# 64-token chunks from the third block on, one pass of K over identity and values, and a new instruction order, in a fused RetNet and RWKV channel-mix kernel

## The chip, the cores and the metric

The kernel runs on one core of one Trainium2 chip. The metric is the device time of one run in microseconds; the median of three runs before the change is 153.27 us (152.85 to 153.36).

## What is computed

Four sequences of 768 tokens with 8 heads of 64 pass through a retention layer, whose output is the input of a gated channel mix (d_model 512, d_ff 1024):

```python
for t in range(S):
    state = gamma[None, :, None, None] * state + np.einsum('bhd,bhe->bhde', k[:, :, t], v[:, :, t])
    y[:, :, t] = scale * np.einsum('bhd,bhde->bhe', q[:, :, t], state)
...
xk = mu_k * x + (1.0 - mu_k) * x_prev
xr = mu_r * x + (1.0 - mu_r) * x_prev
k = np.maximum(xk @ w_k, 0.0)
v = k * k @ w_v
r = 1.0 / (1.0 + np.exp(-(xr @ w_r)))
return (r * v)
```

## The kernel before, in words

The tokens are cut into 12 blocks of 256, three for each sequence. A block's retention is computed in chunks: scores of the tokens of a chunk among themselves (masked), plus what the state carried into the chunk gives, plus the chunk's own addition to the state. Decay is folded into constants: V is scaled once by powers of gamma, and the output is scaled back, so that the masks hold only zeros and ones.

Three sets name how each block is cut. Blocks in `HALF` use four chunks of 64 tokens, with TensorE split into 64x64 quadrants, four of which work at once. Blocks in `WIDE` (2 to 5) use two chunks of 128 tokens, with 64x128 and 128x64 tiles, two at once. Blocks 0 and 1 use 128-token chunks of interleaved tokens. Blocks in `WHOLE` turn (transpose) q and k 128 tokens at a time, the others 64.

**The order is written out.** The scheduler is off. `ORDER` is one list of words; each is a step, its engine (`~v` VectorE, `~a` ScalarE, `~p` GpSimd, `~s` SyncE; none means TensorE or a fixed engine) and the PSUM banks (`@`) of its result. Every engine runs its own words strictly in the order of the list, so a word that waits holds all later words of its engine. GpSimd and SyncE issue the DMAs, in the same way. The first number of a word is the block:

- `lq`, `lk`, `lv` (L223): loads of q, k and v of a block; `wk`, `wr`, `wv`: loads of weights. Input buffers are rings of four blocks. `ck`, `cq`: casts of the first half block.
- `Tq`, `Tk` (L265) and `Eq`, `Ek` (L241, through L285 and L297): TensorE turns q and k into PSUM; ScalarE copies them to SBUF as f16.
- `vs` (L253): V scaled, as f16.
- `S` (L312, L324): scores; `M` (L347, L354): scores times mask.
- `C` (L359, L373): products of K and V, the chunks' additions to the state; `U` (L419): running sums of the state over chunks; `G` (L424): the decay from block to block.
- `I` (L441): the first half of the state's part of the output; `Y` (L456, L470): the scores' part, and for most blocks the second half of the state's part; `J`: that half by itself. They accumulate in the same two banks. `D` (L507, L514): the output, scaled, into `xT`.
- `dx` (L529) and `X.n.w.j` (L558, for block 0 L552 with `t`, L542): difference to the token before, and the two mixes (w = 0 for xk, w = 1 for xr), one for each of four 128-channel slices j.
- `K` (L582, L572), `Qa` (L591), `Qb` (L599, L603): keys, relu, square; `R` (L612), `s` (L618): gate and sigmoid; `V` (L624; `Vc` L642): values; `O` (L630; `Oc` L649): their product; `st`, `sc`: stores.
- `cm` (L680): masks and identity; `gy` (L718, L728): powers of gamma; `mu`, `mt`, `me`: the mix weights; `z` (L703, L710): products of zeros on TensorE that nobody reads.

`GROUPS` joins blocks 3 and 4, 6 and 7, 9 and 10 for the channel mix: their words `X`, `K`, `Qa` and `Qb` (with the first block's number) treat both blocks at once. So `R.10` needs all four `X.9.1.j`, and `K.9.g` all four `X.9.0.j`.

Of the kernel before, what the change touches and what calls it, by code (L numbers as in the profile page):

```python
# [799 lines left out]
```

## Time and profile before

| | |
|---|---|
| median of three runs | 153.27 us |
| span of the profiled execution | 151.4 us |
| TensorE (PE) busy | 143.4 us, 2426 matmuls |
| VectorE (DVE) busy | 127.8 us, 212 instructions |
| ScalarE (ACT) busy | 103.6 us, 195 instructions |
| GpSimd (POOL) busy | 55.3 us, 65 instructions |
| HBM read, written | 24.16 MB, 6.29 MB |

The profiled execution has no time of its own besides its span; the 1.9 us between the span and the median of the timed runs is what lies around the span. PE is the matmuls, PEld the weight loads that run beside them. Matmuls are pipelined and the ends of their bars are modelled, so that what a group of them costs is read from the distance between starts, or from the chain. In a group's row stand line, engine, operation, output <- input, shapes, count, then busy time and mean length of one, then the idle time just ahead of them and what ended it. The chain of work is followed back from the last instruction; a share in it belongs to whatever the end waited for at that time. The tenths show the busy share in 40 equal slices of 3.8 us.

### The profile page before, as it was taken

How to read it: one execution, taken by the hardware profiler on the slowest of the kernel's cores; microseconds unless marked ns; L12 is line 12 of the kernel's file. 1: busy time of each engine (PE TensorE's matmuls, PEld its weight loads, DVE VectorE, ACT ScalarE, POOL GpSimd, SP SyncE). 2: the span in 40 equal slices, each digit the busy share in tenths (PEclk: the TensorE clock that was granted, in tenths of full speed). 3: DMA queues.
4: the chain of work that ended last, by engine and by line, in shares of the span. 5: the costliest groups of instructions: out<-in, count | busy, mean ns of one | idle time of the engine just before them, and what ended most of it. 6: DMA issues, size and time to landing. Idle time of an engine off the chain costs nothing.

```text
span 151.4 us, 5541 instructions
## 1 busy us (share of the span) xinstructions
PE 143.4 (95%) x2426; PEld 82.8 (55%) x2426; DVE 127.8 (84%) x212; ACT 103.6 (68%) x195; POOL 55.3 (37%) x65
## 2 busy tenths in 40 slices
PE   7878799999999999999999999999999999999991
PEld 3345487757754554547465564548456444655450
DVE  7886999999989999999999999999799999400432
ACT  3565979899844795779567786999604756839420
POOL 7953998577957309996710000000000000000000
PEclk9999999999999999999999999999999999999999
DMA  5999999999999999999999019301000005500433
GB/s 140 219 229 197 207 231 192 168 251 212 196 167 202 233 262 107 256 300 198 231 173 126 7 38 283 105 35 45 0 4 0 4 0 211 205 0 0 148 133 139
DMA packets 45624, 22.16 MB, mean 146 GB/s; under 512 B 37400, under 2 KB 41248, under 8 KB 45600
## 3 DMA queue, kind: packets, MB, share of 16 engines
q0 software_dynamic: 38704, 14.42, 74.5%
q1 hardware_dynamic: 6592, 7.21, 14.3%
q8 instruction: 19, 0.31, 0.8%
q10 hardware_dynamic: 304, 0.18, 0.4%
q14 instruction: 5, 0.04, 0.1%
HBM read 24.16 MB, written 6.29 MB: 201 GB/s over the span
## 4 chain that ended last, share of the span: by engine, by line
PE 73%; DMA 12%; POOL 11%; issue 1%; DVE 0%; POOLq 0%
PE ps L624 27%; PE ps L572 14%; DMA v<-in_v_dram 12%; PE ps L612 12%; PE ps L582 8%; PE ps L278 3%; POOL q L235 3%; POOL k L230 2%; PE ps L441 2%; POOL vs L253 2%; POOL v L230 2%; PE ps L366 1%; PE ps L462 1%; PE ps L642 1%; PE ps L318 1%
## 5 line engine op out<-in xcount | busy, mean ns | idle before, releaser
L624 PE MATMUL ps<-wv,k2s 128*128 128x512 f16 x184 | 44.1, 380 | 0.0
L591 ACT ACTIVATE kr<-ps 128x512 f32<-128x512 f32 x48 | 27.9, 594 | 12.5 <-PE ps L582 6.5
L624 PEld LDWEIGHTS <-k2s 128*128 128x128 f16 x184 | 17.1, 98 | 18.9 <-ACT k2s L603 0.4
L630 DVE SCALAR_TENSOR_TENSOR os<-ps,rs 128x512 f32<-128x512 f32 x23 | 15.6, 684 | 11.9 <-ACT rs L618 9.4
L612 PE MATMUL ps<-wr,xr 128*128 128x512 f16 x96 | 23.5, 379 | 0.0
L582 PE MATMUL ps<-xk,wk 128*128 128x256 f16 x192 | 23.2, 273 | 0.0
L572 PE MATMUL ps<-xk,wk 128*128 128x512 f16 x96 | 23.0, 379 | 0.0
L618 ACT ACTIVATE rs<-ps 128x512 f32<-128x512 f32 x24 | 13.6, 597 | 12.9 <-PE ps L612 12.1
L230 POOL DMA_DIRECT2D k<-in_k_dram x20 | 17.8, 903 | 10.3 <-PE ps L384 6.7
L582 PEld LDWEIGHTS <-wk 128*128 128x128 f16 x192 | 18.1, 98 | 3.7
L241 ACT COPY qT<-ps 128x1024 f16<-128x1024 f16 (+1 forms) x13 | 12.3, 946 | 9.5 <-PE ps L278 7.8
L558 DVE SCALAR_TENSOR_TENSOR xr<-dx,mu,xT 128x256 f16<-128x256 f32 (+1 forms) x32 | 17.9, 577 | 0.1
L230 POOL DMA_DIRECT2D v<-in_v_dram x18 | 16.0, 911 | 3.6 <-DMA wr<-in_moe_w_r_dram 1.9
L558 DVE SCALAR_TENSOR_TENSOR xk<-dx,mu,xT 128x256 f16<-128x256 f32 (+1 forms) x32 | 17.0, 579 | 0.2
L354 DVE TENSOR_TENSOR a<-ps,c_sb 128x1024 f16<-128x1024 f32 (+1 forms) x14 | 14.6, 1066 | 0.9 <-PE ps L339 0.6
L603 ACT ACTIVATE k2s<-kr 128x512 f16<-128x512 f32 x24 | 14.8, 631 | 0.3
L612 PEld LDWEIGHTS <-xr 128*128 128x128 f16 x96 | 9.0, 97 | 10.7 <-issue 0.5
L572 PEld LDWEIGHTS <-wk 128*128 128x128 f16 x96 | 9.1, 98 | 10.5
L599 ACT ACTIVATE k2s<-kr 128x512 f16<-128x512 f32 x24 | 14.5, 627 | 0.3
L241 ACT COPY kT<-ps 128x1024 f16<-128x1024 f16 (+1 forms) x13 | 12.2, 945 | 2.2 <-PE ps L272 1.7
L529 DVE TENSOR_TENSOR dx<-xT 128x1024 f32<-128x1024 f32 x11 | 13.4, 1221 | 0.2
L253 DVE TENSOR_TENSOR vs<-v,csm_sb 128x1024 f16<-128x1024 f32 x10 | 12.2, 1217 | 0.2 <-DMA v<-in_v_dram 0.2
(73 smaller groups left out, 165.6 us busy)
## 6 DMA issues: line engine op xcount, KB each, us to landing
out_dram<-os SPq DMA_DIRECT2D x23, 256.0 KB, 2.4
v<-in_v_dram POOLq DMA_DIRECT2D x18, 256.0 KB, 7.7
q<-in_q_dram POOLq DMA_DIRECT2D x11, 256.0 KB, 8.4
k<-in_k_dram POOLq DMA_DIRECT2D x21, 128.0 KB, 8.8
v<-in_v_dram POOLq DMA_DIRECT2D x2, 512.0 KB, 7.2
wk<-in_moe_w_k_dram POOLq DMA_DIRECT2D x2, 512.0 KB, 10.4
...
```

The costliest lines, as they stand in the source:

```text
L230: e.dma_start(out=dst[:, :, i * D : i * D + D], in_=src[:, i * P : i * P + P].rearrange("h p d -> p h d"),)
L241: e.copy(out=out, in_=in_)
L253: e.tensor_tensor(out=VS(n), in0=V32(n).rearrange("p h (i d) -> p i h d", i=2), in1=gks[:, int(half(n) or wide(n)), :, :, None].to_broadca ...
L354: nc.vector.tensor_tensor(out=a_full(n)[:, i, :, j0:j1], in0=pairs(banks("S", n, i, j0))[:, :, j0:j1], in1=(below if wide(n) else causal[: ...
L558: nc.vector.scalar_tensor_tensor(out=XM[w](k)[:, j, t0:t1], in0=DX(k)[:, j, t0:t1], scalar=mu[:, w * NCO + j : w * NCO + j + 1], in1=x[:, ...
L572: nc.tensor.matmul(banks("K", n, g), lhsT=wk16[:, co, g * P : g * P + P], rhs=XM[0](k)[:, co, :], start=(co == 0), stop=(co == NCO - 1),)
L582: nc.tensor.matmul(pz[:, i, :], lhsT=wk16[:, co, fo * P : fo * P + P], rhs=XM[0](k)[:, co, m * TM + t0 : m * TM + t1], start=(i == 0 and c ...
L591: nc.scalar.activation(out=kr, in_=banks("K", n, g, *u), func=AF.Relu)
L603: nc.scalar.activation(out=K2(n)[:, w * g : w * g + w, t0:t1], in_=kr.rearrange("p a t -> p (a t)").rearrange("p (i t) -> p i t", i=w), fu ...
L612: nc.tensor.matmul(banks("R", n, tb), lhsT=XM[1](k)[:, co, t : t + P], rhs=wr16[:, co, :], start=(co == 0), stop=(co == NCO - 1),)
L624: nc.tensor.matmul(banks("V", n, tb), lhsT=K2(n)[:, fo, tb * P : tb * P + P], rhs=wv16[:, fo, :], start=(fo == 0), stop=(fo == NFO - 1),)
L630: nc.vector.scalar_tensor_tensor(out=OS(2 * n + tb), in0=banks("V", n, tb), scalar=1.0 / (KSC * KSC), in1=RS(2 * n + tb), op0=ALU.mult, op ...
```

## The change

Blocks 2 to 5 move into `HALF`: 64-token chunks in quadrants, like the later ones, with no `J` and one mask in place of two, four running sums in place of two, and an output in two pieces. `WIDE` is empty, and `WHOLE` keeps only blocks 0 and 1.

For blocks 2 to 11 (`MERGED`) the words `Tk`, `C` and `Ek` are replaced by `TC.n.i` and `Ec.n.i` (i = 0, 1, the two halves of the chunks). `TC` loads each 64x64 piece of K once as weights and runs 128 columns over it: 64 of an identity that now lies at the front of the buffer of scaled values (`VI`), and 64 of values. One matmul so gives the turned keys and the addition to the state, side by side in f32 PSUM; `Ec` copies the keys' half out, `U` reads the other half. Three identity columns are made in `cm.2`.

A new word `w` (`fence`) lets ScalarE copy a few elements of the banks of `I.n` into a buffer that nobody reads; `Y.n` writes these banks and so waits for it. wk is loaded in three pieces. The order is new throughout; the whole list is replaced, and the diff below shows some stretches of it.

```diff
-HALF = (6, 7, 8, 9, 10, 11)
+HALF = (2, 3, 4, 5, 6, 7, 8, 9, 10, 11)
 EARLY = ((1, 0, 0), (0, 0, 0))
 GROUPS = ((0,), (1,), (2,), (3, 4), (5,), (6, 7), (8,), (9, 10), (11,))
 APART = (0,)
-WHOLE = (0, 1, 2, 3)
-WIDE = (2, 3, 4, 5)
+WHOLE = (0, 1)
+WIDE = ()
+MERGED = (2, 3, 4, 5, 6, 7, 8, 9, 10, 11)
...
-cm.0~v cm.1~v cm.2~v gy.0~v mu~a lv.0~p lq.0.0.2~s lk.0.0.2~s ck.0.0.2~a cq.0.0.2~a z.12@6
-Tq.0.0.2@0 Tk.0.0.2@1 gy.1~v z.1@2 mt@2 Ek.0.0.2~a Eq.0.0.2~a S.0.1.0.2@01 S.0.0.0.2@45 me~a
-lk.0.2.4~p Tk.0.2.4@3 Ek.0.2.4~a lq.0.2.4~p vs.0~v C.0@67 M.0.1.0.2~v U.0.0~v Tq.0.2.4@2 Eq.0.2.4~a
...
-X.8.1.0~v X.8.1.2~v Y.9 D.9~v G.10~a U.11.0~v st.5.0~s U.11.1~v U.11.2~v Qa.8.0~a I.10@23 V.6.1.0@7
-V.6.1.1 O.6.1~v V.6.0.0@4 V.6.0.1 I.11@01 S.11@67 M.11~v dx.9~v V.7.1.0@5 V.7.1.1 Y.10 D.10~v
...
-dx.11~v X.11.1.0~v X.11.1.1~v X.9.1.1~v V.8.1.0@6 K.9.2@3 X.11.0.0~v K.9.6@7 Qa.9.6~a V.8.1.1
-Qa.9.2~a Qb.9.2~a X.11.0.3~v K.9.5@7 K.9.3@3 K.9.0@2 Qa.9.0~a Qb.9.6~a V.8.0.0@0 V.8.0.1 Qb.9.0~a
-Qa.9.5~a Qb.9.5~a Qa.9.3~a O.7.1~v st.7.1~s X.9.1.2~v X.11.0.1~v O.6.0~v K.9.7@1 R.8.1@7 s.8.1~a
-K.9.1@5 R.8.0@7 X.9.1.3~v X.11.0.2~v st.6.1~s O.8.1~v R.9.1@4 R.9.0@6 K.11.0@3 K.11.3@2 s.8.0~a
-Qa.9.1~a Qb.9.1~a Qb.9.3~a V.10.0.0@5 V.9.0.0@7 Qa.11.0~a Qb.11.0~a Qa.11.3~a s.9.0~a K.9.4@6
-R.10.0@2 Qa.9.7~a X.11.1.3~v st.6.0~s K.11.1@1 Qa.11.1~a Qa.9.4~a K.11.2@3 Qb.9.7~a Qb.9.4~a
-Qa.11.2~a X.11.1.2~v O.8.0~v st.7.0~s st.8.1~s st.8.0~s V.9.1.0@1 V.10.1.0@6 s.10.0~a V.9.1.1
-V.10.0.1 s.9.1~a O.9.1~v st.9.1~s Qb.11.2~a Qb.11.3~a O.10.0~v st.10.0~s R.10.1@4 V.9.0.1 s.10.1~a
-O.9.0~v R.11.1@4 V.10.1.1 Qb.11.1~a V.11.0.0@7 R.11.0@5 s.11.0~a st.9.0~s Vc.11.1.1@1 s.11.1~a
-O.10.1~v st.10.1~s Oc.11.1.1~v V.11.0.1 O.11.0~v st.11.0~s sc.11.1.1~a Vc.11.1.0@4 Oc.11.1.0~v
-sc.11.1.0~s
...
+gy.0~v lk.0.0.2~s ck.0.0.2~a cm.2~v cm.0~v gy.1~v lv.0~p cm.1~v z.4@0 z.4@1 z.2@0 Tk.0.0.2@0 mu~a
+lq.0.0.2~s cq.0.0.2~a vs.0~v lq.0.2.4~p lk.0.2.4~p Ek.0.0.2~a Tq.0.0.2@1 Eq.0.0.2~a z.3@7
+S.0.1.0.2@23 Tq.0.2.4@0 Eq.0.2.4~a M.0.1.0.2~v S.0.0.0.2@45 M.0.0.0.2~v Tk.0.2.4@1 C.0@67 U.0.0~v
+Ek.0.2.4~a S.0.1.2.4@23 I.0@01 U.0.1~v w.0~a S.0.0.2.4@45 M.0.1.2.4~v lk.1~p lq.1~p Tk.1@6 Ek.1~a
+lv.1~p z.2@7 Tq.1@2 Eq.1~a wk.0.1~p M.0.0.2.4~v wk.1.2~p Y.0 z.1@3 S.1.1@67 D.0~v G.0~a S.1.0@45
+mt@2 me~a M.1.1~v wk.2.4~p t.0.0.3~a t.0.1.3~a t.0.0.0~a t.0.0.2~a vs.1~p z.4@3 C.1@23 M.1.0~v
+U.1.0~v z.3@7 I.1@01 X.0.0.3~v X.0.0.2~v t.0.1.0~a X.0.0.0~v t.0.0.1~a X.0.0.1~v w.1~a t.0.1.1~a
+U.1.1~v Y.1 lq.2~p z.1@5 K.0.0@4 Qa.0.0~a G.1~a K.0.2@2 Qa.0.2~a t.0.1.2~a D.1~v K.0.3@0 dx.1~v
+X.1.0.1~v Tq.2@67 X.1.0.0~v Eq.2~a X.1.0.3~v lv.2~p X.1.0.2~v vs.2~v X.1.1.0~v Qa.0.3~a X.0.1.0~v
+X.1.1.3~v K.0.1@1 K.1.3@2 lk.2~p Qb.0.0~a wr~p TC.2.0@45 U.2.0~v X.1.1.1~v TC.2.1@67 Ec.2.0~a
+U.2.1~v lv.3~p Qb.0.3~a Ec.2.1~a Qa.0.1~a Qb.0.1~a K.1.0@3 K.1.1@0 Qa.1.0~a S.2@45 Qb.1.0~a
+X.0.1.2~v Qa.1.1~a X.1.1.2~v R.1.1@1 U.2.2~v I.2@67 w.2~a Qa.1.3~a Qb.1.1~a R.1.0@3 s.1.0~a M.2~v
+Y.2 Qb.1.3~a X.0.1.1~v s.1.1~a X.0.1.3~v vs.3~v K.1.2@0 Qa.1.2~a D.2~v dx.2~v lk.3~p TC.3.0@45
...
+X.2.1.2~v TC.4.0@01 wv.0~p lq.5~p Ec.4.0~a D.3~v U.4.0~v TC.4.1@45 U.4.1~v U.4.2~v Ec.4.1~a U.4.3~v
+Qa.2.1~a wv.1~p K.2.3@3 S.4@67 X.2.1.0~v Qb.1.2~a I.4@01 V.1.0.0@2 Qa.2.3~a V.0.0.0@3 w.4~a
+X.2.1.3~v Qb.2.3~a Tq.5@45 M.4~v dx.3~v Y.4 D.4~v X.2.1.1~v V.0.1.0@6 G.4~a V.1.1.0@7 dx.4~v V.1.0.1
...
+K.3.5@0 Qa.3.5~a st.0.0~s Qb.3.5~a X.3.1.2~v D.5~v O.2.0~v dx.5~v X.5.0.1~v K.3.7@6 R.4.1@7 I.6@23
+Qa.3.7~a Qb.3.7~a st.2.0~s s.4.1~a TC.7.0@45 Ec.7.0~a U.7.0~v w.6~a U.7.1~v st.2.1~s TC.7.1@01
+U.7.2~v X.5.0.0~v R.3.0@6 Ec.7.1~a U.7.3~v X.5.0.2~v R.4.0@7 s.3.0~a s.4.0~a Qb.3.0~a R.3.1@4
+X.5.0.3~v Y.6 s.3.1~a Qb.3.2~a lk.8~p D.6~v dx.6~v S.7@67 M.7~v I.7@01 K.5.2@5 K.5.1@4 Qa.5.1~a
+V.3.1.0@2 lv.8~p vs.8~v V.4.1.0@3 w.7~a Y.7 D.7~v dx.7~v X.6.0.2~v lq.10~p Tq.10@67 X.6.0.3~v
...
+Ec.11.0~a Qb.6.5~a K.8.0@2 Qa.8.0~a R.7.1@3 s.7.1~a U.11.0~v st.4.1~s U.11.1~v S.11@45 Qb.6.4~a
+I.10@01 V.6.0.0@2 U.11.2~v I.11@67 w.10~a Y.10 M.11~v I.9@45 X.8.1.2~v w.11~a Y.11 X.8.1.3~v D.10~v
+w.9~a Y.9 K.8.1@3 Qa.8.1~a Qb.8.1~a D.11~v D.9~v dx.9~v V.7.0.0@0 dx.10~v Qb.8.0~a X.9.0.0~v
...
+X.11.0.1~v X.11.0.3~v V.7.1.1 O.6.1~v K.9.3@7 Qa.9.3~a X.11.1.2~v s.8.1~a st.6.1~s K.9.7@5 O.7.1~v
+Qb.9.3~a Qa.9.7~a X.11.0.2~v R.8.0@1 Qb.8.2~a X.9.1.0~v st.7.1~s K.9.4@6 Qb.8.3~a Qa.9.1~a Qb.9.1~a
+K.9.2@5 s.8.0~a X.9.1.1~v st.7.0~s X.9.1.3~v R.10.1@7 R.10.0@2 X.11.0.0~v Qa.9.5~a Qa.9.4~a V.8.1.1
+K.11.1@6 Qa.9.2~a Qb.9.2~a O.8.1~v Qb.9.7~a Qa.11.1~a R.9.1@5 R.9.0@3 V.8.0.1 K.9.6@6 s.9.0~a
+Qb.9.4~a K.9.0@3 X.11.1.3~v Qa.9.0~a K.11.3@0 K.11.0@1 Qb.9.0~a s.10.1~a Qa.9.6~a V.10.0.0@3
+st.6.0~s V.9.1.0@6 O.8.0~v Qa.11.0~a K.11.2@1 st.8.0~s V.9.0.0@4 Qb.9.5~a V.10.1.0@7 X.11.1.1~v
+X.11.1.0~v Qa.11.2~a R.11.1@1 Qb.9.6~a st.8.1~s V.9.1.1 s.10.0~a s.9.1~a O.9.1~v V.9.0.1 V.10.1.1
+O.9.0~v Qb.11.2~a Qa.11.3~a Qb.11.1~a st.9.0~s O.10.1~v st.10.1~s Qb.11.0~a V.11.0.0@0 V.10.0.1
+st.9.1~s R.11.0@2 Qb.11.3~a V.11.0.1 O.10.0~v st.10.0~s Vc.11.1.1@3 Vc.11.1.0@4 s.11.0~a O.11.0~v
+st.11.0~s s.11.1~a Oc.11.1.1~v Oc.11.1.0~v sc.11.1.1~a sc.11.1.0~s
...
+    def VS(n):
+        return VI(n)[:, 1:].rearrange("p (i h) d -> p i h d", i=2)
...
-    VS = ring("vs_", 3, [2, H, D], F16)
+    VI = ring("vs_", 3, [2 * H + 1, D], F16)
...
+    def both(n, i):
+        return banks("TC", n, i).rearrange("p u (j x t) -> p u j x t", j=NJ, x=2)
+
+    def turned_state(e, n, i):
+        ps = both(n, i)
+        for j in range(NJ):
+            for u in range(2):
+                for a, h, jo, hp in heads(j):
+                    k = 1 + i * H + h
+                    x = slice(0, 2) if more(n) or not (u and i) else slice(0, 1)
+                    nc.tensor.matmul(
+                        ps[low(a), u, j, x], lhsT=K16(n)[low(u), h, i * D : i * D + D],
+                        rhs=VI(n)[low(u), 0 : k + 1 : k][:, x],
+                        start=(j == 0), stop=(j == NJ - 1), skip_group_check=True,
+                    )
+
+    def turned_k_part(e, n, i):
+        copy(
+            e, KT(n)[:, :, i].rearrange("c j (u p) -> c u j p", u=2), both(n, i)[:, :, :, 0],
+        )
+
     def carried(n, c):
         return TG[c if half(n) else 2 * c](n)
 
     def summed(e, n, c):
-        src = banks("C", n)
-        if half(n):
-            src = src[:, c % 2, c // 2 * NJ * D : (c // 2 + 1) * NJ * D]
-            last = c == 3
+        last = c == (3 if half(n) else 1)
+        if merged(n):
+            src = both(n, c // 2)[:, c % 2, :, 1]
...
+    def fence(e, n):
+        us = slice(0 if half(n) or not first(n) else 1, 2)
+        e.copy(out=fenced[:, us], in_=pairs(banks("I", n))[:, us, :, 0:C:W])
...
-            ((step, 2, ALU.is_ge), (below, 0, ALU.is_ge)),
+            ((step, 2, ALU.is_ge), (below, 0, ALU.is_ge))
+            + tuple((VI(i)[:, 0], 2, ALU.is_equal) for i in range(3) if MERGED),
...
-    def load_wk(e, h):
-        f = slice(h * dff // 2, (h + 1) * dff // 2)
+    def load_wk(e, a, b):
+        f = slice(a * dff // 4, b * dff // 4)
```

More of the change, by code (lines that the diff above doesn't have):

```diff
@@ L158 @@
     zero = const.tile([P, P], F32, name="zero")
-    mu8 = const.tile([P, P], F32, name="mu8")
+    fenced = const.tile([P, 2, NJ, 2], F32, name="fenced")
     mu = const.tile([P, 2 * NCO], F32, name="mu")
@@ L177 @@
     count = OS(3)[:, 0:P]
+    mu8 = OS(2)[:, 0:P]
     ctx.enter_context(tc.manual_schedule())
@@ L213, in first, with merged @@
         return n % NB == 0
+    def merged(n):
+        return n in MERGED
     def more(n):
```

75 lines of the change are left out of this document (31 added, 44 removed).

## Prediction

> **What bounds the kernel now.** I read the page's totals first, then the busy tenths, then the chain.
>
> ```profile
> span 151.4 us, 5541 instructions
> PE 143.4 (95%) x2426; PEld 82.8 (55%) x2426; DVE 127.8 (84%) x212; ACT 103.6 (68%) x195; POOL 55.3 (37%) x65
> ...
> PE   7878799999999999999999999999999999999991
> ...
> DVE  7886999999989999999999999999799999400432
> ACT  3565979899844795779567786999604756839420
> ...
> PE 73%; DMA 12%; POOL 11%; issue 1%; DVE 0%; POOLq 0%
> ```
>
> The chain names PE for 73% of the span and DVE for nothing. Yet the tenths show DVE as full as PE in nearly every slice until the 33rd, after which it is half idle. So I cut the span where the DVE stretch begins and ends. 19.78 us is where DVE starts D.1, and 127.78 us is where it ends X.9.1.3, the last of the four products that the gate matmuls R.9 and R.10 need. The columns are length, then busy time of PE, PE's weight loads, DVE, ACT and POOL.
>
> ```profile
> 0.00:19.78 19.78, 15.31 (x317) 8.91 (x318) 16.19 (x44) 11.81 (x24) 14.74 (x20) 1.00 1.30 198
> 19.78:127.78 108.00, 107.59 (x1994) 62.54 (x1993) 104.81 (x159) 80.05 (x149) 40.54 (x46) 1.00 0.96 145
> ```
>
> In the middle stretch DVE is busy 104.81 of 108.00 us; only 3.19 us are idle. PE is busy too, but it can put V and R groups, whose inputs are ready long before, wherever it likes. After 127.78 DVE has little left (the zeros and fours that end its line of tenths) and PE works on. The seam shows how tight the two are:
>
> ```profile
> 127.04 0.74 DVE L558 SCALAR_TENSOR_TENSOR xr<-dx,mu,xT 128x512 f16<-128x512 f32 x1
> ```
>
> ```profile
> 127.19 1.89 PE L612 MATMUL ps<-wr,xr 128*128 128x512 f16 x8
> ```
>
> ```profile
> 127.36 2.70 PE ps L612 x12
> ...
> 141.32 0.86 PE ps L624 x4
> ...
> 147.37 0.89 PE ps L642 x8
> ...
> 148.28 0.42 DVE os L649
> ```
>
> The twelve L612 matmuls are R.8.0, R.9.1 and R.9.0 at 0.86 us each, so R.9.1 starts near 127.19 + 0.86 = 128.05, about 0.3 us after its last input. From there PE has 20.2 us left, to 148.26. **Two engines bind, one after the other: DVE up to X.9.1.3, then PE to the end.** A change gains only if it brings this seam forward, or leaves less PE work behind it. The span ends 151.4 - 148.26 = 3.1 us after PE; the median of 153.27 lies 1.9 us above the span. I keep both, since the last two half products and stores are the same.
>
> **PE, part by part.** Dense work is unchanged (the same K, R and V groups). The attention groups change shape:
>
> ```profile
> 56.01 0.55 PE ps L331 x16
> ...
> 60.96 0.57 PE ps L478 x16
> ...
> 70.20 0.38 PE ps L318 x32
> ...
> 95.09 0.38 PE ps L366 x32
> 95.47 0.26 PE ps L318 x32
> ```
>
> ```profile
> 12.60 0.61 PE L272 MATMUL ps<-c_sb,k 128*64 128x128 f16 x16
> 13.14 0.64 PE L489 MATMUL ps<-a,vs 64*64 64x128 f16 x32
> 13.62 0.28 PE L441 MATMUL ps<-qT,tg 64*64 64x128 f16 x4
> ```
>
> A group entered from dense work costs about 0.12 us more than the same behind another small one (0.38 against 0.26). Scores in blocks 2 to 5 go from 0.55 to 0.38, and the value products from 0.57 to about 0.38 (L462 has the shape of L366): 4 x 0.36 = 1.4 us. Transposes in blocks 2 and 3 go from 0.54 (start to start) to 0.26: 4 x 0.28 = 1.1. One pass of K has 32 matmuls of 128 columns at about 0.44 (L489's starts are 0.48 apart with the switch) in place of two passes of 0.26: 0.08 x 10 = 0.8. That is about 3.3 us. The zeros rise from 23 to 24 units of 0.22: -0.2. PE is lighter by about **3.0 us**, bounds 2.1 (no gain in the K pass) and 3.5.
>
> [...]
>
> **DVE up to X.9.1.3.** Durations by form:
>
> ```profile
> L253 DVE TENSOR_TENSOR vs<-v,csm_sb 128x1024 f16<-128x1024 f32 x10 | 12.2, 1217 | 0.2 <-DMA v<-in_v_dram 0.2
> L354 DVE TENSOR_TENSOR a<-ps,c_sb 128x1024 f16<-128x1024 f32 x10 | 12.0, 1219 | 0.3 <-PE ps L331 0.2
> ...
> L419 DVE TENSOR_TENSOR tg<-ps,tg 128x256 f16<-128x256 f32 x20 | 8.4, 418 | 0.6 <-ACT tg L424 0.4
> ...
> L507 DVE TENSOR_TENSOR xT<-ps,gy_sb 128x512 f32<-128x512 f32 x12 | 8.3, 689 | 0.7
> ...
> L514 DVE TENSOR_TENSOR xT<-ps,gy_sb 128x1024 f32<-128x1024 f32 x6 | 7.3, 1218 | 1.4 <-PE ps L441 1.2 <-PE ps L478 0.2
> ...
> L680 DVE TENSOR_SCALAR c_sb<-os,csm_sb 128x64 f16<-128x64 f32 x1 | 0.2, 235 | 0.0
> ```
>
> Blocks 2 to 5 lose one mask each (-4 x 1.22 = -4.88), gain two running sums each (+8 x 0.418 = +3.34), and write their outputs in two pieces instead of one (4 x (2 x 0.689 - 1.218) = +0.64). vs.3 moves from POOL to DVE (+1.22). Three identity columns are new (+0.70). One X.11 moves from before the seam to after it (the 128x256 form, some -0.48). Sum: **+0.5 us**. So the engine that carries the seam is not relieved at all: 121.0 us of work (16.19 + 104.81) become 121.5. One duration has no row: the running sums of merged blocks read 64 columns out of every 128. If that costs nothing, 0.418 holds; were it as dear as a mix of the same 256 elements (0.48), 37 sums would add 2.2 us. I take 0.418, since the output's L507 also walks in strides and costs no more per element than the mask's L354.
>
> What can move the seam is DVE's idle time:
>
> ```profile
> 3.11 1.62 DVE L680 TENSOR_SCALAR c_sb<-os,csm_sb 128x128 f16<-128x128 f32 x5
> ...
> 4.77 2.57 DVE L728 TENSOR_TENSOR gy_sb<-gy_sb,csm_sb 128x4 f32<-128x4 f32 x8
> ...
> 10.87 1.89 DVE L354 TENSOR_TENSOR a<-ps,c_sb 128x512 f16<-128x512 f32 x3 [0.60 <-PE ps L339]
> 13.95 1.23 DVE L514 TENSOR_TENSOR xT<-ps,gy_sb 128x1024 f32<-128x1024 f32 x1 [1.19 <-PE ps L441]
> ...
> 109.88 1.23 DVE L347 TENSOR_TENSOR a<-ps,c_sb 128x1024 f16<-128x1024 f32 x1 [0.72 <-PE ps L318]
> ```
>
> At the start the new order computes powers (L728) before masks (L680). The identity that the first transposes need then comes some 2 us later in DVE's queue, near 6.6 us; but DVE, busy until about 9 us with the same words in any order, needs the first scores no earlier. The four masks of block 0 then stand closer together. Of 0.60 + 1.19 us I let 1.0 go (an estimate; bounds 0 and 1.8). The rest stays, since D.0 still waits for Y.0. The wait of 0.72 goes: S.11 is now issued ahead of V.6.0.0, not behind four V groups. Of the other 2.5 us in the middle stretch I change nothing; bounds are 1.3 gained, and the waits below.
>
> The seam then comes at 127.78 + 0.5 - 1.0 - 0.7 = **126.6**. Behind it the new order has more PE work than the old one: R.10.1, which needs X.9.1.3, and 25 groups after it, 26 x 0.865 = 22.5 us, where 23 groups (20.2 us) stood behind R.9.1. So the lighter PE shows as work that had to be left for the tail, because DVE doesn't come sooner. DVE's rest doesn't break that tail: four products and two results (some 3.3 us) stand before R.11.1's last input, 16 groups (13.8 us) on PE. PE ends at 126.6 + 0.1 + 22.5 = 149.2, the span at 152.3, the run at **154.2 us**, 0.9 above the median.
>
> **What I cost at nothing.** ACT:
>
> ```profile
> L591 ACT ACTIVATE kr<-ps 128x512 f32<-128x512 f32 x48 | 27.9, 594 | 12.5 <-PE ps L582 6.5 <-PE ps L572 6.0
> ...
> L241 ACT COPY kT<-ps 128x1024 f16<-128x1024 f16 x11 | 11.0, 1010 | 0.5 <-PE ps L278 0.5
> ...
> L241 ACT COPY kT<-ps 128x512 f16<-128x512 f16 x2 | 1.2, 586 | 1.7 <-PE ps L272 1.7
> ...
> L694 ACT COPY mu<-ps 128x8 f32<-128x8 f32 x1 | 0.2, 183 | 0.0
> ```
>
> Twenty half copies of keys replace ten whole ones (20 x 0.59 - 10 x 1.01 = +1.8 us; from an f32 source no row shows them, but the f16 form has 0.586 and L591's f32 form 0.594), and twelve fences add 12 x 0.18 = 2.2. ACT's middle stretch goes from 80 to about 84 of 108 us, so the throughput fits. The waits may not. Each fence makes Y.n wait for ACT, and behind Y.n in PE's queue stand dense groups; ahead of the fence in ACT's queue stand squares and copies of 0.6 us. Loads keep their bytes and pieces, only wk comes in three pieces instead of two (+0.8 us of POOL, which loses vs.3's 1.9). V now matters more: the pass over K needs both K and scaled V, where the turned keys needed K alone.
>
> ```profile
> 25.54 10.37 DMA v<-in_v_dram
> ...
> 35.98 1.91 POOL vs L253
> ```
>
> V of block 3 landed at 25.54 + 10.37 = 35.91 with 10 MB queued up to it (blocks 0 to 3, q and k of block 4, wk, wr). The new order queues 8 MB; at the same 0.28 MB per us that is 29 us, in time for its place in DVE's queue near 30.
>
> **Rivals.** (1) *The lighter PE shows.* If it did in full: 153.27 - 3.0 = 150.3. DVE's work forbids that: with 1.8 us gone at the start and all but 1.2 us of the middle's idle time, the seam is at 127.78 + 0.5 - 1.8 - 2.0 = 124.5, so PE ends at 147.1 and the run at 152.1. For it: PE has slack to serve DVE early. Against: three engines are nearly full at once. (2) *Fences stall PE* and so the scores that DVE masks. Between I and Y the order puts dense groups in most blocks, but little in blocks 1, 5, 9 and 11; 4 x 0.5 us (half an ACT instruction, the copy, the way back) = 2.0: 156.2. It decides once ACT runs more than one dense group (0.86 us) behind. (3) *V comes late* in blocks 3 and 4. Keys, copies, scores and mask (0.44 + 0.59 + 0.59 + 0.38 + 1.22 = 3.2 us) then follow it, where they ran beside it; two thirds exposed give 156.3.
>
> **How the numbers follow.** No change means within 0.3%, 152.8 to 153.7, about what a measurement of this kernel can tell. Forecast 50% (faster 2, same 11, slower 37), its own range 153.0 to 155.4. Rival 1 25% (faster 22, same 3), rival 2 18% and rival 3 7% (all slower). Faster 0.24, same 0.14, slower 0.62. The range runs from 151.8 (rival 1 with only 0.9 us idle left in the middle) to 156.4 (rivals 2 and 3).
>
> **What would show it.** Right: DVE still over 95% busy between D.1 and X.9.1.3, the seam at 126 to 127.5, and 22.5 us of unbroken PE behind it. Rival 1: seam before 125. Rival 2: PE or its weight loads waiting for the fence line, several times 0.3 us or more. Rival 3: DVE idle at L253, waiting for V's DMA between 25 and 45 us. Wrong altogether: a seam somewhere else, such as R.10.1 not starting on X.9.1.3, or a DVE instruction whose duration changes with its new strided source in PSUM (the running sums read every second 64 columns).

## The result and the profile after

The changed kernel takes **166.44 us** (median of 4 runs, 165.45 to 168.66), the kernel before 153.28 beside it (152.85 to 153.36). The ratio is 1.084, 95% interval 1.080 to 1.088. Ratios, and differences between two kernels below, leave out runs that are over 1.5% above the fastest of their kernel; medians and ranges are of all runs. The forecast was 154.2 with a range up to 156.4: the sign is right, the size is not, 13.2 us where 0.9 was expected.

The page of the changed kernel (its profiled execution took 166.31 us). First the totals, then four rows of tenths, then the chain by engine:

```profile
span 164.5 us, 5668 instructions
PE 145.8 (89%) x2459; PEld 81.9 (50%) x2459; DVE 129.0 (78%) x224; ACT 103.6 (63%) x217; POOL 54.2 (33%) x65
...
PE   7789728898398999979899999999899999999992
...
DVE  6996759999558998998699999999999997230342
...
PEclk9999999999969999999999999999999999999999
DMA  6999999999999996972999006801100006030063
...
PE 42%; DVE 28%; ACT 11%; issue 10%; DMA 5%; POOL 2%; DVEq 0%; ACTq 0%; POOLq 0%
```

Before, both PE and DVE showed nearly unbroken nines from the sixth slice on. Now both have holes in the first twenty slices, and the chain, which named DVE for nothing, changes hands all the time. "issue", time in which an engine waits for nothing that the profile shows, has grown from 1% to 10%.

Where along the span is the time lost? I cut both executions where D.5 ends and where X.9.1.3 ends (the seam). Columns: length, then busy time of PE, PE's weight loads, DVE, ACT and POOL, granted clock. First before, then after:

```profile
0.00:65.00 65.00, 60.12 (x1120) 36.91 (x1121) 60.43 (x105) 47.86 (x93) 46.43 (x56) 1.00 1.44 205
65.00:127.78 62.78, 62.78 (x1191) 34.54 (x1189) 60.57 (x97) 43.99 (x81) 8.85 (x11) 1.00 0.58 98
```

```profile
0.00:75.70 75.70, 62.49 (x1256) 36.12 (x1257) 62.89 (x120) 48.28 (x104) 46.24 (x56) 0.98 1.38 187
75.70:138.50 62.80, 60.36 (x1076) 33.25 (x1075) 58.88 (x94) 40.50 (x86) 7.93 (x9) 1.00 0.44 91
```

The second stretch is as long as before (62.80 and 62.78 us). **All of the seam's delay, 10.7 us, lies ahead of D.5**, and DVE's idle time there went from 4.6 to 12.8 us; the other 2.5 us are DVE work, most of it done earlier in the new order. (The span has grown by 13.1 us; the other 2.4 lie behind the seam, in the longer tail that was forecast.) Over both stretches DVE works 121.77 us (forecast 121.5) and is idle 16.73 us (before 6.78, forecast about 5).

What does DVE wait for? The list of waits of the changed kernel names the waiting line, the line that ended the wait, total, number and longest:

```profile
DVE tg L452 <- ACT kT L251: 3.8, 6, 1.3
DVE xT L547 <- ACT dx L579: 3.2, 1, 3.2
DVE xT L540 <- PE ps L474: 2.6, 1, 2.6
...
DVE xT L547 <- PE ps L474: 1.4, 1, 1.4
DVE t L452 <- ACT kT L251: 1.0, 2, 0.7
```

In the kernel before, the waits of the same kinds are these:

```profile
DVE xT L514 <- PE ps L441: 1.2, 1, 1.2
...
DVE tg L419 <- ACT tg L424: 0.4, 2, 0.2
DVE xT L514 <- PE ps L478: 0.2, 1, 0.2
```

So three of the new ones have no counterpart. **(a)** D.1 waits 3.2 us for ACT's t.0.1.2. ACT does it last of a short queue:

```profile
20.07 0.60 ACT L628 ACTIVATE kr<-ps 128x512 f32<-128x512 f32 x1 [1.63 <-PE ps L619]
20.56 1.05 ACT L457 ACTIVATE tg<-t,csm_sb 128x64 f16<-128x64 f32 x4
21.52 0.58 ACT L628 ACTIVATE kr<-ps 128x512 f32<-128x512 f32 x1
21.99 0.50 ACT L579 ACTIVATE dx<-xT,nu 128x256 f32<-128x256 f32 x1
```

The new order lists t.0.1.2 behind Qa.0.0, G.1 and Qa.0.2, and ACT takes its words in that order, so Qa.0.0's wait for PE counts as well. D.1 starts at 22.52, as t.0.1.2 ends. (They touch different columns of xT; that the wait is there because their address ranges interleave is argued, not tested.) **(b)** D.3 waits 2.6 us for Y.3 on PE. **(c)** The running sums wait 4.8 us in eight pieces for Ec: ACT copies the turned keys out of the same two banks from which DVE takes the state products, and one waits for the other (ACT waits 7.3 us for L452 in return).

For (b), PE's timeline around Y.3. Columns: start, length, instruction, count, and in brackets the idle time before it:

```profile
42.17 0.44 PE L495 MATMUL ps<-a,vs 64*64 64x64 f16 x32
42.45 0.27 PE L474 MATMUL ps<-qT,tg 64*64 64x64 f16 x8
45.44 0.25 PE L474 MATMUL ps<-qT,tg 64*64 64x64 f16 x4 [2.73 <-issue]
45.62 1.27 PE L619 MATMUL ps<-xk,wk 128*128 128x256 f16 x8
```

PE stops in the middle of one word, between two matmuls of the same tiles, and no engine, DMA or semaphore ends the wait. In that gap the queue of instruction fetches (q8, 19 packets of 16 KB in the span) moves one packet, from 43.09 to 44.03. Behind the gap the clock is halved for 3.4 us:

```profile
46.30:49.70 3.40, 3.40 (x48) 2.04 (x45) 2.14 (x5) 0.59 (x2) 2.47 (x3) 0.50 1.82 175
```

What the forecast had behind the seam held. X.9.1.3 ends at 138.5, R.10.1 starts on it, and PE then runs 22.67 us unbroken (forecast 22.5), to 161.42:

```profile
136.42 2.07 DVE L595 SCALAR_TENSOR_TENSOR xr<-dx,mu,xT 128x512 f16<-128x512 f32 x3
```

```profile
138.75 1.89 PE L649 MATMUL ps<-wr,xr 128*128 128x512 f16 x8
```

### The profile page after: what moved, and what is told of

Same layout as the page of the kernel before. It is cut to its first block, busy times and chain, and to the rows that moved or that the text cites. A ratio compares the mean times of both kernels' runs of the same rounds, so it can differ in the third digit from the quotient of the medians.

```text
span 164.5 us, 5668 instructions
## 1 busy us (share of the span) xinstructions
PE 145.8 (89%) x2459; PEld 81.9 (50%) x2459; DVE 129.0 (78%) x224; ACT 103.6 (63%) x217; POOL 54.2 (33%) x65
## 4 chain that ended last, share of the span: by engine, by line
PE 42%; DVE 28%; ACT 11%; issue 10%; DMA 5%; POOL 2%; DVEq 0%; ACTq 0%; POOLq 0%
PE ps L661 11%; PE ps L609 8%; PE ps L649 6%; PE ps L619 6%; DVE xk L595 6%; DMA q<-in_q_dram 5%; DVE xT L540 4%; ACT kr L628 4%; DVE dx L566 4%; DVE tg L452 4%; DVE xr L595 3%; DVE os L667 3%; DVE vs L263 3%; ACT kT L251 2%; PE ps L474 2%
## 5 line engine op out<-in xcount | busy, mean ns | idle before, releaser
L628 ACT ACTIVATE kr<-ps 128x512 f32<-128x512 f32 x48 | 28.0, 601 | 21.9 <-PE ps L609 15.0
L619 PE MATMUL ps<-xk,wk 128*128 128x256 f16 x192 | 25.2, 280 | 3.3 <-DVE xT L547 2.9
L655 ACT ACTIVATE rs<-ps 128x512 f32<-128x512 f32 x24 | 14.1, 608 | 8.9 <-PE ps L649 4.5
L251 ACT CAST kT<-ps 128x512 f16<-128x512 f32 x20 | 11.9, 599 | 12.4 <-DVE tg L452 7.3
L595 DVE SCALAR_TENSOR_TENSOR xr<-dx,mu,xT 128x256 f16<-128x256 f32 (+1 forms) x32 | 17.8, 577 | 0.0
L540 DVE TENSOR_TENSOR xT<-ps,gy_sb 128x512 f32<-128x512 f32 x20 | 13.8, 691 | 4.3 <-PE ps L474 2.6
L452 DVE TENSOR_TENSOR tg<-ps,tg 128x256 f16<-128x256 f32 x28 | 11.8, 422 | 4.6 <-ACT kT L251 3.8
L649 PEld LDWEIGHTS <-xr 128*128 128x128 f16 x96 | 9.0, 97 | 10.2 <-issue 0.2
L566 DVE TENSOR_TENSOR dx<-xT 128x1024 f32<-128x1024 f32 x11 | 13.3, 1221 | 0.2
## 6 DMA issues: line engine op xcount, KB each, us to landing
wv<-in_moe_w_v_dram POOLq DMA_DIRECT2D x2, 512.0 KB, 10.7
```

Of the source, the lines that this page charges most:

```text
L251: e.copy(out=out, in_=in_)
L452: nc.vector.tensor_tensor(out=to, in0=src, in1=carried(n, c), op=ALU.add)
L540: nc.vector.tensor_tensor(out=x[:, :, :, v], in0=banks("I", n)[:, v].rearrange("p (j i t) -> p j i t", j=NJ, i=2), in1=g[:, :, :, v], op=A ...
L566: e.tensor_tensor(out=DX(k)[:, :, m * TM + t0 : m * TM + t1], in0=x[:, :, c + t0 : c + t1], in1=x[:, :, c - 1 + t0 : c - 1 + t1], op=ALU.s ...
L595: nc.vector.scalar_tensor_tensor(out=XM[w](k)[:, j, t0:t1], in0=DX(k)[:, j, t0:t1], scalar=mu[:, w * NCO + j : w * NCO + j + 1], in1=x[:, ...
L619: nc.tensor.matmul(pz[:, i, :], lhsT=wk16[:, co, fo * P : fo * P + P], rhs=XM[0](k)[:, co, m * TM + t0 : m * TM + t1], start=(i == 0 and c ...
```

## The experiments

**Theory 1**: the loss is a sum of single stands that the new order and its small matmuls bring. Within it, **1a**: PE runs through its program in pages of 16 KB, 256 instructions or 128 matmuls with their weight loads; where small matmuls use a page up sooner than the next one can come, PE stands. **1b**: what stops PE lies in Y.3 itself. **Theory 2**: the shared banks (c) are the loss, or the new parts are, wherever they stand. (In e2's expectation, 1b stands for a fetch that is late because of data transfers.)

The first four ran once each, on the same chip as a run of the kernel before (152.92).

**e1**, for (a): one word moved.

```diff
-w.1~a t.0.1.1~a U.1.1~v Y.1 ... G.1~a K.0.2@2 Qa.0.2~a t.0.1.2~a D.1~v
+w.1~a t.0.1.1~a t.0.1.2~a U.1.1~v Y.1 ... G.1~a K.0.2@2 Qa.0.2~a D.1~v
```

> The changed kernel with one word moved: t.0.1.2, a ScalarE product of block 0, goes ahead of the first relu instead of behind two relus and a decay. In the changed kernel D.1 waits 3.2 us for it on DVE, and a K group on PE then waits 2.9 us for D.1. Theory 1 (the loss is a sum of single waits of the new order, each of which holds DVE): the run falls by 2.5 to 3.2 us, to about 163.5, and D.1 starts near 19.4 us instead of 22.5. Theory 2 (the loss comes from the shared PSUM banks of keys and state products alone, and DVE makes up for early idle time later): D.1 starts earlier, but the run stays within 1 us of 166.4.

165.23 us, 1.1 below the changed kernel's profiled run, but only 0.2 below the shortest of its runs. In the traces the seam comes 1.1 us sooner. D.1 follows at once now, 3.16 us sooner (both rows are e1's):

```profile
19.36 1.22 DVE L547 TENSOR_TENSOR xT<-ps,gy_sb 128x1024 f32<-128x1024 f32 x1
```

```profile
43.47 0.32 PE L474 MATMUL ps<-qT,tg 64*64 64x64 f16 x4 [3.12 <-issue]
```

but PE, sooner at the same place in Y.3, stands there 3.12 us instead of 2.73 (all its stands of this kind add up to 5.7 us instead of 4.4), and only 1.1 us are left of the 3.2.

**e2**, for (b): Tq.4 (32 small matmuls ahead of Y.3) moved behind K.2.1.

```diff
-s.0.1~a Tq.4@45 S.3@01 K.2.2@2 ... Y.3 K.2.1@2 Eq.4~a
+s.0.1~a S.3@01 K.2.2@2 ... Y.3 K.2.1@2 Tq.4@45 Eq.4~a
```

> The changed kernel with one word moved: Tq.4 (32 small transposes) goes from ahead of S.3 to behind Y.3 and the K group after it, so that fewer small matmuls stand close together ahead of Y.3, where PE stands still for 2.7 us with no wait while its next 16 KB of instructions are fetched, and then runs 3.4 us at half the clock. Theory 1a (too many small matmuls in a row outrun the fetch): the gap goes, no half clock, the run falls by 2.5 to 4 us, to about 163. Theory 1b (the fetch is late because data transfers fill the DMA engines): a gap of 1 us or more stays somewhere between 38 and 48 us and the run stays within 1 us of 166.4.

165.81 us. The stand in Y.3 is gone; 0.70 us of one are now inside Tq.4, but the copy of the queries and Ec come later and hold PE up for 0.89 us ahead of TC.4.1 and 1.48 us in S.4, and from 48.4 us on the clock is at 0.50 again, for 3.4 us. Neither expectation came whole: the stands fell from 4.4 to 1.8 us in all, as 1a had it, and the time by only 0.5.

**e3**, for (c): each Ec right behind its TC.

```diff
-TC.2.0@45 U.2.0~v X.1.1.1~v TC.2.1@67 Ec.2.0~a U.2.1~v ... Ec.2.1~a
+TC.2.0@45 Ec.2.0~a U.2.0~v X.1.1.1~v TC.2.1@67 Ec.2.1~a U.2.1~v
...
```

> The changed kernel with every Ec.n.i moved right behind its TC.n.i, ahead of the running sums U that read the same PSUM banks. Theory 2 (keys wait for DVE to reach the sums, because copy and sum of one bank are put one after the other): ScalarE's wait for the sums (7.3 us in the changed kernel) goes nearly to zero, scores and masks come earlier, and the run falls by 2 to 4 us. Theory 1 (DVE's own idle time is what counts): DVE's waits for the copies (4.8 us) grow instead, and the run moves by less than 1 us or gets slower by up to 2.

167.35 us, 0.9 us above the changed kernel's median and within its range. ACT's 7.3 us of waits for L452 are gone from its list, and DVE's waits for Ec fell from 4.8 to 2.1 us (theory 1 had them grow), yet PE now stands 3.66 us in Y.3:

```profile
47.05 0.25 PE L474 MATMUL ps<-qT,tg 64*64 64x64 f16 x4 [3.66 <-issue]
```

**e4** and **e7**: the new order without the merged pass. Tk and C stand where the two TC stood, one Ek for two Ec. In e4 two running sums (U.6.3 and U.11.2) read a bank that has been written again, so that part of what it computes is not the operation's; e7 has them a few words earlier.

```diff
-MERGED = (2, 3, 4, 5, 6, 7, 8, 9, 10, 11)
+MERGED = ()
...
-TC.3.0@45 ... U.3.0~a Ec.3.0~a U.3.1~v ... TC.3.1@67 Ec.3.1~a
+Tk.3@45 ... Ek.3~a ... C.3@67 U.3.0~a U.3.1~v
```

> The changed kernel and its order, but with the merged pass undone: TC.n.0 and TC.n.1 become Tk.n and C.n in the same banks, one whole copy Ek takes the place of the two Ec, and the sums that stood ahead of the second TC follow C. Keys and state products no longer share banks. Theory 2: DVE's waits for the copies and ScalarE's waits for the sums vanish (4.8 and 7.3 us); with 0.8 us more of PE the run falls by 3 to 5 us, to 162 or 163. Theory 1: the wait of D.1 and the gap at Y.3 stay, and the run falls by 0 to 2 us.

> The new order without the merged pass, as e4, with two running sums (U.6.3 and U.11.2) a few words earlier so that each reads its bank before it is written again. Theory 1a: 288 matmuls more than after, so again stands at pages' ends, 8 us or more in sum, and 171 to 176 us. If e4's time came from the two displaced sums: 166 to 169 us.

173.87 and 173.46 us (before beside e7 153.21). That is where theory 1a put e7. With 288 matmuls more than the changed kernel, its stands of this kind add up to 9.9 us (two of them here):

```profile
45.81 0.28 PE L472 MATMUL ps<-qT,tg 64*64 64x64 f16 x9 [1.42 <-issue]
...
52.82 0.23 PE L374 MATMUL ps<-vs,k 64*64 64x64 f16 x5 [3.68 <-issue]
```

So by itself the merged pass is a help in this order, 7 us; that it helps because it saves matmuls fits the stands, but is argued.

**f1**: the old order with 64-token chunks in blocks 2 to 5, their fences, and nothing else of the new order.

```diff
-S.3.1@67 M.3.1~v S.3.0@01 vs.3~p C.3@23 U.3.0~a ... I.3@45 ... U.3.1~v ... M.3.0~v ... J.3
+S.3@67 M.3~v vs.3~p C.3@23 U.3.0~a U.3.1~v U.3.2~v ... I.3@45 w.3~a ... U.3.3~v
...
```

> The kernel before, its order of words kept, with 64-token chunks in blocks 2 to 5 alone (one score word, one mask and three or four running sums for each block, fences w.2 to w.5, no J, no merged pass). DVE's work by the rows of before: four masks of 1.22 us fewer, eight running sums of 0.42 us more, four outputs in two halves (+0.16 each), so -0.9 us. Theory 1 (what is lost lies in the new order, not in the new parts): 151.5 to 153.5 us, the seam within 1 us of 127. Theory 2 (the small matmuls and the fences of the new parts stall PE, wherever they stand): over 156 us, with DVE idle 4 us or more longer ahead of the seam than the 6.8 us of before.

162.93 us, ratio 1.064 (1.061 to 1.068): theory 1 as I had put it, "the loss lies in the new order", misses by 10 us, and theory 2's case for f1 came. From D.1 to the seam, now at 137.94, DVE does the work of before (104.9 us, before 104.8) and is idle 13.3 us instead of 3.2:

```profile
19.80:137.94 118.14, 109.48 (x2250) 63.26 (x2249) 104.87 (x167) 80.52 (x153) 40.29 (x45) 0.99 0.88 133
```

So these parts alone, in the old order, delay the seam by 10.2 us, nearly as much as the whole change. D.2 starts 0.5 us later than before (31.59 against 31.07), D.3 8.1 later (52.14 against 44.07). Between them PE stands twice in the middle of a word, 3.9 us in all; how much of the rest is the half clock behind the second stand or the longer chain of running sums stays open:

```profile
35.55 0.29 PE L326 MATMUL ps<-qT,kT 64*64 64x64 f16 x12
37.66 0.35 PE L326 MATMUL ps<-qT,kT 64*64 64x64 f16 x20 [1.82 <-issue]
...
41.09 0.40 PE L374 MATMUL ps<-vs,k 64*64 64x64 f16 x28
43.59 0.25 PE L374 MATMUL ps<-vs,k 64*64 64x64 f16 x4 [2.10 <-issue]
```

**f2**: the old order with the merged pass in blocks 8 to 11 alone.

```diff
-Tk.9@23 Ek.9~a ... vs.9~v ... C.9@23 ... U.9.0~a
+vs.9~v ... TC.9.0@23 TC.9.1@45 Ec.9.0~a Ec.9.1~a ... U.9.0~a
...
```

> The kernel before, its order kept, with the merged pass of K in blocks 8 to 11 alone: TC and Ec stand where C stood (their second halves next to the running sums that read them), the turning of K by itself goes. Theory 1 (the order is the loss): within 1.5 us of before, 152 to 154.5 us, for DVE's work is unchanged. Theory 2 (copies on ACT and running sums on DVE that share banks hold each other up, 12.1 us of waits in ten blocks after): four blocks bring DVE some 2 us of waits at L452, and 155 us or more.

172.46 us (1.123 to 1.131). Neither theory gives 19 us. In my placing the keys are turned only where C stood, so each score and its mask come that much later, and the fitted order around them waits: DVE waits 7.3 us for scores at the mask and 9.8 us for the results V, where before had 0.9 and 2.3. It tells what such a placing costs, not what the merged pass costs.

**g1**: the place of the pages. Two of the opening's zero matmuls give way to 32 small ones, so every later word stands 30 matmuls further on in its page.

```diff
-z.4@0 z.4@1 z.2@0 Tk.0.0.2@0
+z.4@0 z.4@1 zt.32@0 Tk.0.0.2@0
```

> The changed kernel with one edit: two of the opening's zero matmuls give way to 32 small ones (128 rows, 32 columns), so that all of PE's instructions behind them stand 60 places later in their 256-instruction pages, and no page up to 100 us is used up in under 4.6 us (the changed kernel has one of 3.3 and one of 1.7 us). Theory 1a (PE stands for the fetch of its instructions): the stand of 2.73 us in Y.3 and that of 1.18 us at 73 us both go, the half clock from 46.3 to 49.7 us too, and 1.5 to 3 us of the time. Theory 1b (PE stands for something in Y.3 itself, the fetch only falls there): the stand stays in Y.3, and the time within 0.5 us of 166.4.

168.15 us (166.99 to 169.90). The time went against 1a's number (1.7 us more, not 1.5 to 3 less): the stands didn't go, those of over 1 us now add up to 5.8 us. But they moved just as 1a has it:

```profile
43.29 0.28 PE L495 MATMUL ps<-a,vs 64*64 64x64 f16 x10
44.84 0.38 PE L495 MATMUL ps<-a,vs 64*64 64x64 f16 x22 [1.27 <-issue]
45.02 0.32 PE L474 MATMUL ps<-qT,tg 64*64 64x64 f16 x12
...
46.25 0.64 PE L423 MATMUL ps<-vs,k 64*64 64x128 f16 x32
46.82 1.05 PE L619 MATMUL ps<-xk,wk 128*128 128x256 f16 x8
...
49.78 0.30 PE L474 MATMUL ps<-qT,tg 64*64 64x64 f16 x14
51.85 0.22 PE L474 MATMUL ps<-qT,tg 64*64 64x64 f16 x2 [1.77 <-issue]
```

In the changed kernel PE stood with 4 of L474's 12 matmuls to go; now it stands 30 matmuls earlier, between the 10th and 11th of L495 (22 + 8 = 30), and L474's 12 follow without a pause. A new stand has come one page later. **What stops PE is the count of instructions, not the word.** The same holds for every kernel here that has such stands. The table gives how many matmuls PE had done in all when one began (the long ones of some kernels; in no trace does a stand for "issue" of over 0.4 us fall elsewhere):

| kernel | matmuls done before each stand (its length, us) |
|---|---|
| changed | 607 (0.50), 735 (2.73), 1246 (1.18) |
| e1 | 607 (1.22), 735 (3.12), 1246 (1.37) |
| e7 | 606 (1.76), 734 (1.42), 862 (3.68), 2526 (1.96) |
| f1 | 606 (1.82), 734 (2.10), 1502 (1.04) |
| g1 | 223 (1.17), 735 (1.27), 863 (1.77), 2270 (1.60) |
| i1; i2 (below) | 606 (3.59); 2142 (1.05) |

Every number leaves a remainder of 94 or 95 when divided by 128: the stands are whole pages apart, whatever the word.

**g2**: the same with t.0.1.2 moved as in e1.

> The same edit, with t.0.1.2 moved ahead of Qa.0.0 as in e1 as well. If single stands add up (theory 1): 1.1 us, what that move brought by itself, to 3 us less than g1, so that 161 to 164 us are left. If one stand only covers another, no more than 0.5 us less than g1.

166.79 us (165.65 to 168.94): 1.4 less than g1. That is theory 1's difference at its low end; its 161 to 164 us were missed, since g1 had not fallen.

**h1**: f1 with its pages shifted by some 75 matmuls.

```diff
-z.12@6 Tq.0.0.2@0 Tk.0.0.2@1
+z.4@6 zt.80@6 Tq.0.0.2@0 Tk.0.0.2@1
```

> f1 (162.9 us) with its pages shifted: two thirds of the opening's twelve-fold zeros give way to 80 small zero matmuls, so that PE's instructions stand some 150 places later in their pages, and the pages between 25 and 50 us are used up in 5 to 6 us each instead of one of 3.6. Theory 1a (PE stands at the end of a page until the next has come): f1's stands of 2.03 us at 37.7 and 2.31 us at 43.6 go or shrink to 1 us at most, the half clock behind them goes, D.3 ends at 47 to 49 us instead of 52.8, and the time is 157 to 160 us. If the 8 us between D.2 and D.3 are the longer chain of running sums (G.3, three sums, I.4) or lost cover: 162 us or more, with D.3 still past 51.

169.76 us (165.67 to 171.44). A miss: with the 80 small zeros the opening was late (D.0 starts at 16.82 us, in f1 at 13.94; the clock was at 0.50 from 7.6 to 17.8 us), and stands came after 606, 1630 and 1758 matmuls (the same remainder), 1.95, 1.37 and 2.73 us. It says nothing of the price.

**i1** and **i2** measure that price with nothing of the change in the kernel: before, with one page of small zero matmuls at two places.

```diff
-Y.2 Qa.1.3~a
+Y.2 zt.128@5 Qa.1.3~a
```

```diff
-Y.9 D.9~v
+Y.9 zt.128@7 D.9~v
```

> The kernel before, nothing of the change in it, with 128 small zero matmuls (64 rows, 64 columns, one page of 256 PE instructions) behind Y.2, at some 30 us, where the DMA engines are busy. By themselves they take 1 to 2 us. Theory 1a: PE passes the page from 30.4 us on at once, must wait for the next one, which in the trace of before comes 3.0 us after and 0.95 + 1.4 us until PE goes on, so a stand of 3 us or more at a page's end, and a run 3 to 6 us over before. Without a fetch limit: no stand of over 0.5 us at a page's end, and at most 2 us over before.

> The same 128 matmuls behind Y.9, at some 105 us, where the DMA engines are nearly idle. Theory 1a with a fetch that comes after 0.6 to 0.9 us there: a stand of 1 to 2 us at a page's end, and 1 to 3 us over before, less than i1. Without a fetch limit: as i1, at most 2 us over before and no stand.

i1 takes 160.24 us, ratio 1.042 (1.035 to 1.048), 6.4 us over before; i2 156.69, ratio 1.023 (1.021 to 1.025), 3.6 over. Both stands came as 1a has them, and both times lie 0.4 to 0.6 us above its ranges. The zeros keep PE for 2.2 us in i1. i1's stand is seen best in the timeline of PE's weight loads:

```profile
32.98 0.10 PEld L278 LDWEIGHTS <-k 64*64 64x64 f16 x1 [0.42 <-issue]
36.64 0.33 PEld L278 LDWEIGHTS <-k 64*64 64x64 f16 x31 [3.56 <-issue]
```

Tk.4's first weights are loaded at 32.98, so K has come; its first matmul and the other 31 loads come 3.6 us later. (The list of waits names a load of V, which Tk.4 doesn't read and which lands at that moment; had K been late, the first weights couldn't have been loaded.) A page is fetched in between, from 34.03 to 35.35, and the clock behind it is 0.50 from 37.32 to 40.74 us. In i2 the stand is short, and the clock stays at 1.00:

```profile
105.56 1.68 PE L720 MATMUL ps<-zero 64*64 64x64 f16 x95
108.29 0.66 PE L720 MATMUL ps<-zero 64*64 64x64 f16 x31 [1.05 <-issue]
```

The difference is the delay of the fetch. Counting by the same remainder, at the stands ahead of 55 us, where the DMA engines' tenths show nines (the changed kernel, e1, e7, f1, g1, i1), the packet of q8 starts 3.0 to 4.8 us after PE has entered the page that it then uses up; at i2's stand, where they show mostly zeros, 0.7 us after. The packet takes 0.9 to 1.3 us, and at each of these stands PE goes on 1.2 to 1.5 us after it has landed. So PE spends 5.3 to 7.0 us on a page that ends in a stand early, and 3.0 us in i2. In the trace of before no page up to 70 us is used up in less than 5.4 us, and PE's matmuls at a page's end start at most 0.31 us apart: it just fits.

The Trainium skill (Runtime: NRT & Kernel Launch, Instruction fetch mechanics) has the pages too, 16 KB blocks of 256 instructions, but calls the cost of passing from one to the next mostly hidden, since instructions are issued more slowly than they come. With matmuls of 64 columns in four tiles, 8 ns each (32 in 0.26 us), the runs disagree: up to 3.95 us a time (e4).

**j1** and **j2** thin the pages out. The queries of blocks 2 to 7 are turned in 16 matmuls instead of 32 (j1); j2 also has t.0.1.2 moved.

```diff
-WHOLE = (0, 1)
+WHOLE = (0, 1, 2, 3, 4, 5, 6, 7)
...
-Tq.3@01
+Tq.3@0
```

> The changed kernel with the queries of blocks 2 to 7 turned in 16 matmuls of a whole 128-token tile each, as blocks 0 and 1 are, instead of 32 of half a tile (the trace of before has 0.62 us for the one and 0.43 us for the other). 96 matmuls fewer, three quarters of a page, half of them between 30 and 53 us, at 0.2 us of PE's time more for each block. Theory 1a (the fetch limits PE there to a page in 5.5 to 6.2 us): the stand of 2.95 us at 45.4 us shrinks, by up to 2 us, and the time to 163 to 165.5 us. Without the fetch limit: 166.4 us or up to 1 us more.

> The same, with t.0.1.2 ahead of Qa.0.0 as in e1. If e1 won only 1.1 of its 3.2 us because PE came sooner to the same end of a page: with pages that last longer the move now brings 1.5 to 3 us beside j1, 161 to 163.5 us. If not: again 1 us or less.

j1 166.72 (1.078 to 1.092), j2 163.35 us (1.060 to 1.071). Thinning by itself brings nothing that can be told; but on top of it the move of t.0.1.2 is worth 3.1 us, where it was worth 1.1 in e1 and 1.4 in g2. That the page limit had swallowed the difference fits, but is not shown: in the two profiled executions, of 165.08 us each (the shortest of j1's, the longest of j2's), the seam comes at 136.53 us alike, and j2's stands add up to 5.1 us where j1's are 4.2.

**j3** and **j4**: the new order with the parts of before (128-token chunks, keys turned by themselves) in blocks 2 to 5; j4 has t.0.1.2 moved too.

```diff
-HALF = (2, 3, 4, 5, 6, 7, 8, 9, 10, 11)
+HALF = (6, 7, 8, 9, 10, 11)
...
-TC.3.0@45 ... TC.3.1@67 ... S.3@01 ... M.3~v
+Tk.3@4 ... C.3@67 U.3.0~a U.3.1~v ... S.3.1@01 S.3.0@35 ... M.3.1~v M.3.0~v
```

> The new order with blocks 2 to 5 computed as in the kernel before (128-token chunks, two masks, one or two running sums, keys turned by themselves, J), so with fewer and larger matmuls from 25 to 65 us; blocks 6 to 11 and the opening as in the changed kernel. Theory 1a: no stand of over 1 us at a page's end ahead of 60 us, none of the sharing of banks there, and 156 to 161 us. If the loss lies in the new order of the words itself: 163 us or more.

> The same, with t.0.1.2 ahead of Qa.0.0. Theory 1 (with PE free of the pages' ends, what DVE waits ahead of D.1 is on the path): 2 to 3.2 us less than j3. Otherwise within 1 us of it.

167.70 and 165.08 us. Nothing stands at a page's end ahead of 88 us, as expected, and the time is no better, as the other case had it (the loss lies in the new order of the words). DVE is idle 15.9 us ahead of the seam (16.7 in the changed kernel): PE waits for masks and gate inputs (2.3 and 1.4 us), DVE 2.5 us for scores, in places where four more masks and their banks had to be squeezed into an order made for other parts. The move in j4 is worth 3.0 us.

**k1** and **k2** start from j2: k1 puts each Ec right behind its TC as in e3, k2 turns the queries of blocks 8 to 11 in whole tiles too.

> j2 (163.35 us) with each copy of turned keys Ec right behind its TC, so that ACT reads the shared banks ahead of DVE's running sums. If the waits of DVE for Ec (4.6 us at L452 in the changed kernel, 3.3 us of it for the copies in j2) are on the path: 1.5 to 3 us less than j2, 160.5 to 162 us. If the order of the two readers only moves the wait (as e3 had it, 1 us slower): 163 us or more.

> j2 with the queries of blocks 8 to 11 turned in whole tiles too (64 matmuls fewer between 75 and 125 us, where the DMA engines are nearly idle). Theory 1a: the stand of 2.3 us at 121 us moves or shrinks, but DVE's work, not PE's, sets the seam there: within 1 us of j2.

k1 166.53 us: 2.1 us slower than j2, so this order of the two readers only moves the wait. k2 163.05, as expected. Its profiled execution (161.21 us, the shortest of four) is the best account of what was repaired. Window up to its seam, then its waits:

```profile
0.00:133.43 133.43, 123.26 (x2170) 70.29 (x2171) 121.81 (x212) 89.08 (x190) 54.24 (x65) 1.00 0.98 149
```

```profile
DVE tg L452 <- ACT kT L251: 2.2, 6, 0.7
DVE a L357 <- PE ps L328: 1.3, 2, 1.0
...
DVE t L452 <- ACT kT L251: 1.0, 2, 0.7
```

DVE does the same 121.8 us of work; its idle time is 11.6 us instead of 16.7, the seam comes 5.1 us sooner, and the span is 5.1 us shorter (159.4). So of the 9.9 us of idle time that the change brought, the move of t.0.1.2 and the thinner pages together took back 5.1 in this execution, and 3.7 us of the kernel's time. How much each gave isn't separated; k2's stands still add up to 3.8 us, 0.6 less than in the changed kernel. Of the other 4.8 us, 3.2 are waits of the sums for Ec.

## Why the prediction was wrong

- **Two engines bind, DVE up to the seam, then PE**: right. R.10.1 starts on X.9.1.3, and seam and span move together between the changed kernel and k2 (5.1 and 5.1 us).
- **PE's 22.5 us behind the seam**: right (22.67).
- **DVE's work +0.5 us**: right (121.77 against 121.5). The running sums with their strided source take 0.422 us (taken: 0.418).
- **The wait of M.11 goes**: right. **1.0 us less idle time at the start**: 0.4; D.0 still waits 1.42 us.
- **PE lighter by 3.0 us**: wrong, if without effect on the seam. PE's busy time rose from 143.4 to 145.8. 1.7 of it is the half clock (3.40 us at 0.50), and a pair of TC takes 0.57 us from start to start (g1) where I had 0.44, 1.3 us in ten blocks; the remainder I did not settle.
- **Copies and fences on ACT cost nothing by throughput**: right in size (0.599 and 0.173 us each).
- **"Of the other 2.5 us in the middle stretch I change nothing"**: this is the step that failed. I took the idle time of a new order over from the old one. In place of 3.19 us from D.1 to the seam and 3.59 before D.1 there were 10.6 and 6.2, so that DVE was 91% busy between D.1 and the seam, where over 95% was the sign of being right; the seam came at 138.5, not 126.6. "The waits may not" fit, I had written of ACT, and then looked for them only at the fences and at V. Neither rival 2 (PE waited for a fence once, 0.3 us) nor rival 3 (no wait of DVE for V) came. What came instead are t.0.1.2 behind two matmul-fed words in ACT's queue, which could be read off the order; Ec and U in the same banks, which could be read off the diff; and the pages, which no row of before showed as a wait.
- The sign was right mostly by luck. The forecast had the seam 1.2 us earlier and was slower for the longer tail alone; that tail came (2.4 us of the span's 13.1), but the seam came 10.7 us later, and that part it had the wrong way. What it had right is that a lighter PE can't show while DVE carries the seam.

What stays open: how much of the 13.2 us each part has. (a) is worth 1.1 to 1.4 us in the new order as it stands and 3.0 to 3.1 beside other edits (j2, j4). That the stands cost time is shown in i1 and i2; their share here is not: e2 had 1.8 us of them in place of 4.4 and j3 none ahead of 88 us, and neither was faster by over 0.5 us. That the shared banks cost their 4.8 us is argued from the waits alone, and e3, with 2.1 of them left, was no faster. Nor do the two halves of the change add up: 64-token chunks in the old order (f1) bring 10.0 us of DVE idle time, the new order with the old chunks in blocks 2 to 5 (j3) 9.1, and both together 9.9. So in these runs either half is enough to lose what the old order had. The best version found (k2) is still 9.6 us slower than the kernel before, which remains the best.
